# One w_mod tile kept on chip, and eleven row tiles of the up and gate gradients in other places: an adaLN decoder block, forward and backward

## The chip, the core and the metric

The kernel runs on one core of a Trainium2 chip. Its engines are PE (TensorE: matmuls and transposes), DVE (VectorE), ACT (ScalarE), POOL (GpSimd) and SP (SyncE). In this kernel POOL computes next to nothing: it issues most of the transfers between DRAM and SBUF, in program order, and SP issues the rest. The time is that of one execution on the device in microseconds; three executions are given, and their median is the figure.

## The reference, cut to what matters

One token (batch 1, sequence 1, D = 1024) goes through a block whose norms are modulated by a condition vector c, and all gradients are returned beside the output.

```python
mod = (silu(c) @ w_mod).reshape(1, 6, 1, -1)          # w_mod: 1024 x 6144
sa, ca, ga, sb, cb, gb = (mod[:, i] for i in range(6))
h = layernorm(x) * (1 + ca) + sa
x = x + ga * attention(h, k_cache, v_cache, wq, wo)    # 32 heads on 4 kv heads, last 4096 of 65536 positions
h = layernorm(x) * (1 + cb) + sb
x = x + gb * ((sigmoid(h @ w_gate) * (h @ w_up)) @ w_down)   # F = 3584
out, vjp = jax.vjp(f, A_x, k_cache, v_cache, wq, wo, w_gate, w_up, w_down, c, w_mod)
return (out, *vjp(grad_out))
```

The results are the output, a row for x and for c, and full gradients of k_cache, v_cache (1 x 4 x 65536 x 128 each, zero but for the last 4096 positions), wq (1024 x 4096), wo (4096 x 1024), w_up and w_gate (1024 x 3584 each), w_down (3584 x 1024) and w_mod (1024 x 6144), all in bf16. Most of these are outer products of two vectors, made on chip and written out.

## The kernel before, in words

**Storage.** One tile, `arena` (192 KiB of each of the 128 partitions), holds everything large. `ar(off, size)` is a piece of it by KiB; such an offset is called a place here. Every place is used several times in the course of the kernel, and an instruction that writes to a place waits until the earlier readers of those bytes, a store to DRAM among them, are done. Small vectors are tiles of their own, from `vt` (L107). `zeros` (L114) is a 2 KiB tile that feeds the first fills with zeros, `junk`, `scr` and `b1k` are 2 KiB tiles of scratch. `ones_f` (L126) is a 128 x 128 matrix of ones, the stationary operand of the sums over partitions in `total_bcast` (L289) and `layernorm_bwd_col` (L318); c_ps (L1382) reads one column of it.

**Order.** The schedule is written by hand (`manual_schedule`): each engine runs its instructions in program order. Transfers issued by POOL run in one queue, those by SP in another; both share the 16 transfer engines. The zero regions of the k_cache and v_cache gradients, most of the volume written, are cut into pieces of about 1 MB, and `zero(n, after)` puts n of them into POOL's queue, in the N loop and the B chunks each tied to a recent matmul, so that they go out at the matmuls' pace. The tables `Z_...` at the top say how many stand where. None is left after L1328.

**Stages.** w_mod's first two sections, k, wq and v are loaded; scores, softmax and the attention follow. The N loop (L720) runs 128 steps s, four groups of 32: every second step DVE scales two blocks of v, PE multiplies with k. The B chunks (`bch`) multiply with wo, which stays on chip as `wo_t` (places 160, 168, 176, 184, 64, 72, 80, 88). Then the modulations ga, cb, sb and gb are made from sections of w_mod, the FFN runs over seven blocks of F, forward and backward (`turn`, L1143), and the tail makes and stores the gradients.

**gb and its tiles.** Section 5 of w_mod (gb) is used twice: for gb itself, gb = silu(c) @ section 5, and at the end for the gradient of c, in `sec` (L1252). Its eight tiles `g_t[j]` (128 x 1024 bf16, 0.25 MiB each) are at places 48 to 58 for j = 0 to 5; j = 6 goes into the tile `zeros` at step s = 40, once the fills read their zeros from DRAM. For j = 7 there was no place that stays free: it is loaded to place 160 before the N loop (L561), its share of gb is summed at s = 24 and s = 26 (`mod_gb((7,))`, L744, and `gb_cols`, L747), and then wo_t[0] is loaded over it. The shares of the other seven follow at L1028 and are added. In the tail `sec_load(7)` (L1400) loads the tile a second time, into the last quarter of `sec_t[7]`, between sec(3) and sec(4).

**Row tiles.** `dw_rows(k, j, off, outer)` (L1123) makes one row tile of the gradient of w_up (k = 0) or w_gate (k = 1): DVE multiplies dug_row[k] by the column h2[:, j] into 7 KiB at place off, and POOL stores the 896 KiB. There are sixteen, from L1206 to L1397. Between them stand `dwo(u)` (L1258), which writes the gradient of wo over wo_t[u], and `sec(j)`, which makes 8 KiB of w_mod's gradient at the place of `sec_t[j]` (0, 8, 152, 16, 32, 40, 48, 56). Behind them `grad_kv` makes the gradients of v at places 64 to 95 and of k at 96 to 127, `dwq_tile` those of wq at places 184, 0, 8, 152, 32, 40, 16, 48, and `s2` those of w_mod's first two sections at 164, 24, 28, 56, 60, 168, 172, 128.

Of the kernel before, what the change touches and what calls it, by code (L numbers as in the profile page):

```python
# [10 lines left out]
P = 128  # L11
# [8 lines left out]
D = 1024  # L20
# [41 lines left out]
def kernel(  # L62
# [40 lines left out]
    def ar(off, size):  # L103
        return arena[:, int(off * KIB):int((off + size) * KIB)]


    def vt(shape, name, dt=FP32):  # L107
        return pool.tile(shape, dt, name=name)

    ctx.enter_context(tc.manual_schedule())  # L110

# [11 lines left out]
    ident_f = vt([P, P], "ident_f")  # L123
    make_identity(nc, ident_bf)
    make_identity(nc, ident_f)
    ones_f = vt([P, P], "ones_f")  # L126
    nc.vector.memset(ones_f, 1.0)

    def fill_rows(og, g):
# [158 lines left out]

    def total_bcast(part, ncol, name, scale):  # L289
        ps = new_acc("tot_" + name)  # L290
        nc.tensor.matmul(ps[:, 0:ncol], lhsT=ones_f[:, :], rhs=part[:, 0:ncol], start=True, stop=True)
        tot = vt([P, ncol], name)
        ts(tot, ps[:, 0:ncol], float(scale), ALU.mult)
        return tot
# [23 lines left out]
    def layernorm_bwd_col(dln, ln, rstd, name, gap=lambda: None):  # L318
        part = vt([P, 2], name + "_parts")
        nc.vector.reduce_sum(out=part[:, 0:1], in_=dln, axis=AX.X)  # L320
        tmp = vt([P, KD], name + "_tmp")
        ttr(tmp, dln, ln, part[:, 1:2])
        ps = new_acc("tot_" + name)
        nc.tensor.matmul(ps[:, 0:2], lhsT=ones_f[:, :], rhs=part[:, 0:2], start=True, stop=True)
# [52 lines left out]
    def wm_sec(sct, j, n, off, eng=nc.gpsimd):  # L377
        eng.dma_start(out=ar(off, 2 * n).rearrange("p (j x) -> p j x", j=n),
                            in_=wm_view[:, j:j + n, sct * D:(sct + 1) * D])
# [64 lines left out]
    def heads(w):  # L444
        return w.rearrange("p (n d) -> p n d", d=P)
# [105 lines left out]
    for ch in range(8):  # L551
# [5 lines left out]
        nc.scalar.copy(out=P_bf[:, ch * 512:(ch + 1) * 512], in_=ps[:, :])  # L557
        nc.vector.reduce_max(out=mx8[:, ch:ch + 1], in_=ps[:, :], axis=AX.X)
        zero(Z_KC[ch], mm)
    g_t = [ar(o, 2) for o in (48, 50, 52, 54, 56, 58)] + [zeros.bitcast(BF16), ar(160, 2)]  # L560
    wm_sec(5, 7, 1, 160)  # L561
    load_wo(2)
    load_wo(1)
    mx = vt([P, 1], "mx")
# [131 lines left out]
    jobs.clear()  # L696

    dffn_bf = vt([P, KD], "dffn_bf", BF16)
    gb_rest = vt([P, KD], "gb_rest")

    def mod_gb(ts_):
        ps = new_bank("g_ps")
        for t in ts_:
            rows_mm(ps, cs_bf[:, t:t + 1], heads(g_t[t]), t == ts_[0], t == ts_[-1])

        def cols():
            rows_to_cols(gb if ts_[0] == 7 else gb_rest, ps, KD, b1k)
            if ts_[0] != 7:
                addv(gb, gb, gb_rest)
        return cols  # L710

    ok4 = ok_sums()

# [6 lines left out]
    for g in range(G):  # L720
        nbank = bank_pair("n_ps", g)
        for t_ in range(KT):
            s = g * KT + t_
            vp = vp_t[(s // 2) % 2]
            if t_ % 2 == 0:
                tt(vp.rearrange("p t h d -> p (t h d)"),
                   v_nat[:, g, t_ * DH:(t_ + 2) * DH].rearrange("p (t o d) -> p t o d", t=2, o=1).broadcast_to([P, 2, HG, DH]),
                   pT2[:, g, HG * t_:HG * t_ + 2 * HG, :].rearrange("p n (o k) -> p n o k", o=1).broadcast_to([P, 2 * HG, 64, 2]),
                   ALU.mult)
            for k in range(2):  # L730
                mm = nc.tensor.matmul(nbank[k][:, :], lhsT=k_nat[:, g, t_ * DH:(t_ + 1) * DH],  # L731
                                      rhs=vp[:, t_ % 2, 4 * k:4 * k + 4, :].rearrange("p h d -> p (h d)"),
                                      start=(t_ == 0), stop=False)
            zero(Z_N[s], recent(mm, 6), True)
            if t_ == 20:
                build_bd(g)
            if s == 2:
                ok_cols(ok4)
            elif s == 4:
                ok_rows()  # L740
            elif s == 6:
                shuffle_o()
            elif s == 24:
                gb_cols = mod_gb((7,))  # L744
                load_wo(0)
            elif s == 26:
                gb_cols()  # L747
            elif s == 40:
                nc.gpsimd.dma_start(out=g_t[6], in_=wm_view[:, 6, 5 * D:6 * D])
# [275 lines left out]
    assert not bq  # L1025
    park(4, ppq, "pq")
    zero(Z_FOLD[1])
    mod_gb((0, 1, 2, 3, 4, 5, 6))()  # L1028
    mulv(dffn_bf, go_col, gb)
    bcast(dffn_bf, KD, b1k, "AV")  # L1030
    vT_unit = [tr_unit(v_nat[:, i // 4, (i % 4) * 1024:(i % 4 + 1) * 1024]) for i in range(16)]
# [10 lines left out]
    nc.vector.memset(fg, 0.0)  # L1042
    gu_ps, ffn_ps, dh2_ps = fg[:, 0:256], fg[:, 256:256 + KD], fg[:, 272:272 + JT]
    ffn = vt([P, KD], "ffn")
    gu_t = gb_rest

    def ffn_rows(out, col, w, stop):
        for a in range(4):
# [197 lines left out]
    dcs = vt([P, KD], "dcs")  # L1246
    late = [junk[:, i * P:(i + 1) * P] for i in range(8)]

    def sec_load(j):
        nc.gpsimd.dma_start(out=sec_t[j][:, 3 * D:4 * D], in_=wm_view[:, j, 5 * D:6 * D])  # L1250

    def sec(j):  # L1252
        w5 = g_t[j] if j < 7 else sec_t[j][:, 3 * D:4 * D]
        ttr(w5, w5, dmod_b4[:, 3 * D:4 * D], dcs[:, j:j + 1])
        outer_dve(sec_t[j], cs_col[:, j:j + 1], dmod_b4)
        nc.gpsimd.dma_start(out=dwm_view[:, j, 2 * D:6 * D], in_=sec_t[j])
# [78 lines left out]
    for h in range(HQ):  # L1335
        nc.tensor.matmul(dq_ps[:, h:h + 1], lhsT=N_sb[:, h * P:(h + 1) * P], rhs=do_bf[:, h:h + 1], start=True, stop=True)
    dwo(5)
    dq_bf = vt([P, HQ], "dq_bf", BF16)
    cp(dq_bf, dq_ps[:, 0:HQ])
    dug_rows(1)  # L1340
# [3 lines left out]
    dw_rows(0, 4, 32, outer_dve)  # L1344
    zero(Z_ROWS[2])
    dwo(3)
    dw_rows(0, 5, 64, outer_dve)
    dw_rows(0, 6, 72, outer_dve)
    zero(Z_ROWS[3])
    dw_rows(0, 7, 80, outer_dve)  # L1350
    for p in range(5):
        nc.scalar.copy(out=B_t[p], in_=BT_ps[p][:, :])
    dh1_ps = new_acc("dh1_ps")
# [4 lines left out]
    rot[:] = [(psum, "mm"), (pna, "na"), (pgu, "gu"), (ppq, "pq"), (px, "x"), (pna, "na"), (prq, "rq")]  # L1358
    nrot[0] = len(rot) - 1
    bcast(dmod_bf[:, 16:48], 32, dmod_b4, "A")  # L1360
    dw_rows(1, 0, 88, outer_dve)
    zero(Z_ROWS[4])
    dw_rows(1, 1, 40, outer_dve)
    dwo(1)
    dh1 = vt([P, KD], "dh1")
    cp(dh1[:, 0:NBP], dh1_ps[:, 0:NBP])
# [6 lines left out]
    dw_rows(1, 2, 16, outer_dve)  # L1373
    zero(Z_ROWS[5])
    dw_rows(1, 3, 32, outer_dve)
# [8 lines left out]
    crow = vt([P, 1], "crow")  # L1384
    cp(crow, c_ps[:, 0:1])
    sec(0)
    dw_rows(1, 4, 40, outer_dve)
    zero(Z_ROWS[6])
    sec(1)
    dw_rows(1, 5, 16, outer_dve)  # L1390
    for run in vT_unit[12:]:
        run()
    rebuild_P()
    bcast(dq_bf, HQ, dq_b, "A")
    dw_rows(1, 6, 32, outer_dve)
# [115 lines left out]
```

## Time and profile before

| | us |
|---|---|
| three executions | 593.43, 594.07, 594.16 |
| median | 594.07 |
| the profiled execution | 593.93 |
| its span, first to last instruction | 592.1 |

| engine | busy us | share of the span | instructions |
|---|---|---|---|
| PE, matmuls | 421.1 | 71% | 4167 |
| PE, weight loads | 243.2 | 41% | 4196 |
| DVE | 354.7 | 60% | 647 |
| ACT | 248.0 | 42% | 398 |
| POOL | 151.4 | 26% | 251 |

All times in the views are microseconds from the start of the span. The DMA share is the mean busy share of the 16 transfer engines; packets of two queues overlap in the records, so that it can be over 1. "A <- B" behind an instruction means that it stood idle until B was done. The time to landing of a transfer runs from its issue to its last completion, the time in the queue with it. Matmul ends are modelled, and a few per cent of the matmul records can be missing.

### The profile page before, as it was taken

Reading aid. Unit: us, or ns where it says so; the run is one execution under the profiler, and the core shown is the slowest. Engines: PE = TensorE matmul, PEld = TensorE weight load, DVE = VectorE, ACT = ScalarE, POOL = GpSimd, SP = SyncE. Lnnn points to the kernel's source line nnn. Section 1 sums busy time; section 2 is a strip of 40 time slices with the busy share of each in tenths; the row PEclk is TensorE's granted clock in tenths of the full one; section 3 lists DMA queues with packets and bytes.
Section 4 is the critical chain, followed back from the end, with each engine's and each line's share of the span. In section 5 each row is a group of like instructions: output and inputs, shape, how many; then the busy total and the mean of one; then the engine's idle time right before and its main releaser. Section 6 shows DMA issues by size and latency. Waiting matters only on the chain.

```text
span 592.1 us, 10185 instructions
## 1 busy us (share of the span) xinstructions
PE 421.1 (71%) x4167; PEld 243.2 (41%) x4196; DVE 354.7 (60%) x647; ACT 248.0 (42%) x398; POOL 151.4 (26%) x251
## 2 busy tenths in 40 slices
PE   3997679999999999997976756776665408275410
PEld 2784433322334545543444545555452307113100
DVE  3665679988830102039372876887986826696750
ACT  2579511554540103411123655666671426464310
POOL 3113213122122212122232321334222813133100
PEclk9998889999999999999997767778777657755555
DMA  8999999999999999999999999999999999999997
GB/s 347 423 418 422 424 462 427 425 431 425 426 401 452 419 445 426 408 419 438 427 390 407 418 411 408 399 410 402 422 420 427 424 427 421 424 404 413 412 415 321
DMA packets 31983, 246.32 MB, mean 416 GB/s; under 512 B 4781, under 2 KB 4781, under 8 KB 16624
## 3 DMA queue, kind: packets, MB, share of 16 engines
q0 software_dynamic: 26944, 226.25, 94.9%
q1 hardware_dynamic: 4944, 19.41, 9.4%
q8 instruction: 33, 0.54, 0.4%
q14 instruction: 14, 0.11, 0.1%
q10 hardware_dynamic: 48, 0.01, 0.0%
HBM read 88.78 MB, written 185.60 MB: 463 GB/s over the span
## 4 chain that ended last, share of the span: by engine, by line
DMA 34%; PE 26%; DVE 17%; issue 9%; ACT 8%; POOL 2%; ACTq 0%; POOLq 0%; DVEq 0%
DMA out_dram<-out_dram 13%; DMA out_dram<-arena 9%; PE n_ps L731 9%; DMA arena<-in_w_mod_dram 6%; DMA arena<-in_B_w_gate_dram 5%; DVE arena L246 4%; PE b_ps L792 4%; PE t_ps L679 4%; DVE scr L246 3%; DVE arena L242 3%; ACT arena L1295 2%; ACT arena L517 2%; DVE arena L229 2%; ACT arena L687 1%; PE tp_k L496 1%
## 5 line engine op out<-in xcount | busy, mean ns | idle before, releaser
L792 PE MATMUL b_ps<-arena 128*128 128x512 bf16 x493 | 114.3, 379 | 2.4 <-ACT arena L936 1.1
L229 DVE TENSOR_TENSOR arena<-arena 128x2048 bf16<-128x2048 bf16 x64 | 77.7, 1224 | 9.0 <-PE n_ps L731 5.3
L936 ACT COPY arena<-tp_side 128x1024 bf16<-128x1024 bf16 x62 | 60.9, 1017 | 49.7 <-PE tp_side L935 49.0
L792 PEld LDWEIGHTS <-arena 128*128 128x128 bf16 x512 | 48.3, 98 | 56.6 <-issue 2.9
L731 PE MATMUL n_ps<-arena 128*128 128x512 bf16 x246 | 66.2, 388 | 4.1 <-DVE arena L229 3.4
L193 POOL DMA_DIRECT2D out_dram<-out_dram x72 | 35.7, 496 | 127.2 <-PE n_ps L731 50.8
L935 PE MATMUL tp_side<-ident_bf,arena 128*128 128x128 bf16 x496 | 50.5, 268 | 10.2 <-DVE arena L229 5.8
L935 PEld LDWEIGHTS <-arena 128*128 128x128 bf16 x496 | 41.8, 123 | 19.1 <-issue 9.0
L687 ACT CAST arena<-t_ps 128x512 bf16<-128x512 f32 x56 | 28.9, 598 | 39.9 <-PE t_ps L679 39.9
L242 DVE TENSOR_SCALAR arena<-arena,h 128x3584 bf16<-128x3584 bf16 (+1 forms) x24 | 28.5, 1193 | 25.0 <-DMA out_dram<-arena 25.0
L1291 PE MATMUL ps_kv<-arena 32*128 32x512 bf16 x64 | 24.4, 588 | 24.9 <-DVE arena L250 14.4
L246 DVE CUSTOM_DVE_ANT_0 arena<-arena,scr 128x1024 bf16<-128x1024 bf16 x35 | 40.8, 1219 | 0.2
L1295 ACT ACTIVATE arena<-ps_kv 128x512 bf16<-128x512 f32 x48 | 25.4, 697 | 33.2 <-PE ps_kv L1291 33.0
L246 DVE CUSTOM_DVE_ANT_0 scr<-arena,b1k 128x1024 bf16<-128x1024 bf16 x28 | 34.2, 1222 | 3.4 <-DMA arena<-in_B_w_down_dram 3.0
L731 PEld LDWEIGHTS <-arena 128*128 128x128 bf16 x256 | 21.4, 99 | 35.8 <-issue 19.4
L238 DVE CAST arena<-b_ps 128x512 bf16<-128x512 f32 x6 | 4.1, 691 | 48.8 <-PE b_ps L792 48.8
L200 POOL DMA_DIRECT2D out_dram<-out_dram x32 | 19.5, 610 | 32.6 <-DVE rows_all L229 24.4
L679 PE MATMUL t_ps<-arena 128*32 128x512 bf16 x256 | 24.1, 399 | 3.4 <-ACT arena L756 2.8
L517 ACT COPY arena<-tp_wq 128x1024 bf16<-128x1024 bf16 x23 | 21.4, 1070 | 7.3 <-PE tp_wq L515 7.3
L1291 PEld LDWEIGHTS <-arena 32*128 32x128 bf16 x64 | 6.9, 116 | 41.1 <-issue 40.4
L1073 ACT COPY arena<-tp_ug 128x1024 bf16<-128x1024 bf16 x21 | 20.5, 1007 | 7.0 <-PE tp_ug L1072 7.0
L961 POOL DMA_DIRECT2D arena<-in_B_w_up_dram x14 | 10.8, 771 | 39.6 <-DVE dh2acc L246 21.1
(330 smaller groups left out, 671.8 us busy)
## 6 DMA issues: line engine op xcount, KB each, us to landing
out_dram<-arena POOLq DMA_DIRECT2D x35, 1024.0 KB, 12.2
out_dram<-out_dram POOLq DMA_DIRECT2D x32, 1024.0 KB, 12.8
out_dram<-arena POOLq DMA_DIRECT2D x16, 896.0 KB, 12.7
out_dram<-zeros POOLq DMA_DIRECT2D x10, 1024.0 KB, 10.7
arena<-in_A_wq_dram POOLq DMA_DIRECT2D x8, 1024.0 KB, 21.1
arena<-in_A_wo_dram POOLq DMA_DIRECT2D x8, 1024.0 KB, 13.5
arena<-in_w_mod_dram POOLq DMA_DIRECT2D x7, 1024.0 KB, 18.9
arena<-in_B_w_up_dram POOLq DMA_DIRECT2D x14, 512.0 KB, 9.8
```

Of the source, the lines that this page charges most:

```text
L193: ins = nc.gpsimd.dma_start(out=as_rows(region, BIGP).bitcast(FP32), in_=zero_src[:, 0:P * ZW // 4].rearrange("i (p x) -> (i p) x", p=BIGP ...
L229: return nc.vector.tensor_tensor(out=out, in0=a, in1=b, op=op)
L242: return nc.vector.tensor_scalar(out=out, in0=a, scalar1=s1, scalar2=None, op0=op0)
L246: return nc.vector.tensor_tensor_reduce(out=out, in0=w, in1=b, scale=1.0, scalar=0.0, op0=ALU.mult, op1=ALU.add, accum_out=acc)
L517: nc.scalar.copy(out=blk, in_=tp[:, :])
L679: nc.tensor.matmul(ps[32 * hh:32 * hh + 32, :].rearrange("p (j m) -> p j m", j=4), lhsT=N_sb[:, h * P + a:(h + 1) * P - 3 + a:4], rhs=a4[: ...
L687: nc.scalar.copy(out=o, in_=v)
L731: mm = nc.tensor.matmul(nbank[k][:, :], lhsT=k_nat[:, g, t_ * DH:(t_ + 1) * DH], rhs=vp[:, t_ % 2, 4 * k:4 * k + 4, :].rearrange("p h d -> ...
L792: mm = nc.tensor.matmul(bbank[p][k][:, :], lhsT=a4[:, p, h, :], rhs=wo_t[u][:, a, k * 512:(k + 1) * 512], start=(i == 0 and a == 0), stop= ...
L935: nc.tensor.transpose(tp[:, i * P:(i + 1) * P], blk[:, i * P:(i + 1) * P], ident_bf[:, :])
L936: nc.scalar.copy(out=blk if dst is None else dst, in_=tp[:, :])
L1295: nc.scalar.activation(out=o, in_=v, func=ACT.Copy, scale=float(scale))
```

## The change

- `vt` gives vectors of at most 48 words out of one tile, `slab` (728 fp32 words), one behind the other; larger ones stay tiles of their own. Before the last vectors of the tail the slab is set anew to 1.75 KiB at place 146.25.
- `ones_f` is one column, read as a 128 x 128 matrix by a repeated column.
- `g_t[7]` is a tile of its own, `g_last`. Its load before the N loop and `sec_load(7)` go, and it is loaded in the N loop at s = 44.
- `mod_gb` sums all eight tiles at once, where it summed seven; the part at s = 24 and 26 goes. `gu_t`, which shared a tile with the partial sum, has one of its own.
- Eleven of the sixteen row tiles are made in other places. The order of the instructions stays.

| row tile | 0,5 | 0,6 | 0,7 | 1,0 | 1,1 | 1,2 | 1,3 | 1,4 | 1,5 | 1,6 | 1,7 |
|---|---|---|---|---|---|---|---|---|---|---|---|
| place before | 64 | 72 | 80 | 88 | 40 | 16 | 32 | 40 | 16 | 32 | 40 |
| place after | 176 | 160 | 40 | 64 | 72 | 80 | 16 | 32 | 88 | 160 | 40 |

```diff
+    slab = [pool.tile([P, 728], FP32, name="slab"), 0]
     def vt(shape, name, dt=FP32):
-        return pool.tile(shape, dt, name=name)
+        n = shape[1] if dt == FP32 else (shape[1] + 1) // 2
+        if dt not in (FP32, BF16) or n > 48:
+            return pool.tile(shape, dt, name=name)
+        a = slab[1]
+        slab[1] += n
+        v = slab[0][:, a:a + n]
+        return v if dt == FP32 else v.bitcast(BF16)[:, 0:shape[1]]
...
-    ones_f = vt([P, P], "ones_f")
+    ones_f = vt([P, 1], "ones_f")
...
-        nc.tensor.matmul(ps[:, 0:ncol], lhsT=ones_f[:, :], rhs=part[:, 0:ncol], start=True, stop=True)
+        nc.tensor.matmul(ps[:, 0:ncol], lhsT=ones_f[:, 0:1].broadcast_to([P, P]), rhs=part[:, 0:ncol], start=True, stop=True)
...
-    g_t = [ar(o, 2) for o in (48, 50, 52, 54, 56, 58)] + [zeros.bitcast(BF16), ar(160, 2)]
-    wm_sec(5, 7, 1, 160)
+    g_t = [ar(o, 2) for o in (48, 50, 52, 54, 56, 58)] + [zeros.bitcast(BF16), vt([P, D], "g_last", BF16)]
...
-    def mod_gb(ts_):
+    def mod_gb():
         ps = new_bank("g_ps")
-        for t in ts_:
-            rows_mm(ps, cs_bf[:, t:t + 1], heads(g_t[t]), t == ts_[0], t == ts_[-1])
-
-        def cols():
-            rows_to_cols(gb if ts_[0] == 7 else gb_rest, ps, KD, b1k)
-            if ts_[0] != 7:
-                addv(gb, gb, gb_rest)
-        return cols
+        for t in range(KD):
+            rows_mm(ps, cs_bf[:, t:t + 1], heads(g_t[t]), t == 0, t == KD - 1)
+        rows_to_cols(gb, ps, KD, b1k)
...
             elif s == 24:
-                gb_cols = mod_gb((7,))
                 load_wo(0)
-            elif s == 26:
-                gb_cols()
-            elif s == 40:
-                nc.gpsimd.dma_start(out=g_t[6], in_=wm_view[:, 6, 5 * D:6 * D])
+            elif s in (40, 44):
+                j = 6 + (s - 40) // 4
+                nc.gpsimd.dma_start(out=g_t[j], in_=wm_view[:, j, 5 * D:6 * D])
...
-    mod_gb((0, 1, 2, 3, 4, 5, 6))()
+    mod_gb()
...
-    gu_t = gb_rest
+    gu_t = vt([P, KD], "gu_t")
...
-    def sec_load(j):
-        nc.gpsimd.dma_start(out=sec_t[j][:, 3 * D:4 * D], in_=wm_view[:, j, 5 * D:6 * D])
-
     def sec(j):
-        w5 = g_t[j] if j < 7 else sec_t[j][:, 3 * D:4 * D]
+        w5 = g_t[j]
...
     dwo(5)
+    slab[:] = [ar(146.25, 1.75).bitcast(FP32), 0]
...
-    dw_rows(0, 5, 64, outer_dve)
-    dw_rows(0, 6, 72, outer_dve)
+    dw_rows(0, 5, 176, outer_dve)
+    dw_rows(0, 6, 160, outer_dve)
     zero(Z_ROWS[3])
-    dw_rows(0, 7, 80, outer_dve)
+    dw_rows(0, 7, 40, outer_dve)
...
-    dw_rows(1, 0, 88, outer_dve)
+    dw_rows(1, 0, 64, outer_dve)
     zero(Z_ROWS[4])
-    dw_rows(1, 1, 40, outer_dve)
+    dw_rows(1, 1, 72, outer_dve)
...
     sec(3)
-    sec_load(7)
```

More of the change, by code (lines that the diff above doesn't have):

```diff
@@ L104, in ar @@
         return arena[:, int(off * KIB):int((off + size) * KIB)]
+    slab = [pool.tile([P, 728], FP32, name="slab"), 0]
     def vt(shape, name, dt=FP32):
-        return pool.tile(shape, dt, name=name)
+        n = shape[1] if dt == FP32 else (shape[1] + 1) // 2
[3 more added lines that the diff above has]
+        slab[1] += n
+        assert slab[1] <= slab[0].shape[1], slab
+        v = slab[0][:, a:a + n]
+        return v if dt == FP32 else v.bitcast(BF16)[:, 0:shape[1]]
     ctx.enter_context(tc.manual_schedule())
@@ L323, in layernorm_bwd_col @@
         ps = new_acc("tot_" + name)
-        nc.tensor.matmul(ps[:, 0:2], lhsT=ones_f[:, :], rhs=part[:, 0:2], start=True, stop=True)
+        nc.tensor.matmul(ps[:, 0:2], lhsT=ones_f[:, 0:1].broadcast_to([P, P]), rhs=part[:, 0:2], start=True, stop=True)
         gap()
@@ L698 @@
     dffn_bf = vt([P, KD], "dffn_bf", BF16)
-    gb_rest = vt([P, KD], "gb_rest")
-    def mod_gb(ts_):
+    def mod_gb():
         ps = new_bank("g_ps")
-        for t in ts_:
-            rows_mm(ps, cs_bf[:, t:t + 1], heads(g_t[t]), t == ts_[0], t == ts_[-1])
-        def cols():
-            rows_to_cols(gb if ts_[0] == 7 else gb_rest, ps, KD, b1k)
-            if ts_[0] != 7:
-                addv(gb, gb, gb_rest)
-        return cols
+        for t in range(KD):
+            rows_mm(ps, cs_bf[:, t:t + 1], heads(g_t[t]), t == 0, t == KD - 1)
+        rows_to_cols(gb, ps, KD, b1k)
     ok4 = ok_sums()
@@ L1372 @@
     pd = b1k.bitcast(FP32)[:, 0:HQ]
-    dw_rows(1, 2, 16, outer_dve)
+    dw_rows(1, 2, 80, outer_dve)
     zero(Z_ROWS[5])
-    dw_rows(1, 3, 32, outer_dve)
+    dw_rows(1, 3, 16, outer_dve)
     dcs234 = matvec_T(lambda jb, nb: w2_t[jb][:, nb * P:(nb + 1) * P], dh2_hl, "dcs234")
@@ L1386 @@
     sec(0)
-    dw_rows(1, 4, 40, outer_dve)
+    dw_rows(1, 4, 32, outer_dve)
     zero(Z_ROWS[6])
     sec(1)
-    dw_rows(1, 5, 16, outer_dve)
+    dw_rows(1, 5, 88, outer_dve)
     for run in vT_unit[12:]:
@@ L1394 @@
     bcast(dq_bf, HQ, dq_b, "A")
-    dw_rows(1, 6, 32, outer_dve)
+    dw_rows(1, 6, 160, outer_dve)
     zero(Z_ROWS[7])
```

## The prediction

> **What bounds the kernel now.** I read the page first: the span, and the volume that the DMA engines moved. Then a table of stretches, for the busy time of each engine, the DMA share and the rate.
>
> ```profile
> span 592.1 us, 10185 instructions
> ...
> DMA packets 31983, 246.32 MB, mean 416 GB/s; under 512 B 4781, under 2 KB 4781, under 8 KB 16624
> ```
> ```profile
> core 0: us, PE busy (x) PEld busy (x) DVE busy (x) ACT busy (x) POOL busy (x), PEclk, DMA share, GB/s
> 60.00:200.00 140.00, 126.91 (x838) 49.96 (x856) 92.16 (x106) 51.90 (x124) 32.36 (x62) 0.97 1.05 428
> 200.00:330.00 130.00, 111.92 (x933) 61.52 (x936) 48.86 (x105) 33.55 (x43) 32.12 (x55) 0.97 1.04 422
> 330.00:440.00 110.00, 75.46 (x1108) 61.16 (x1109) 88.22 (x184) 66.95 (x88) 32.41 (x49) 0.72 1.14 410
> 440.00:496.00 56.00, 23.35 (x358) 18.04 (x357) 37.09 (x92) 21.46 (x27) 23.70 (x26) 0.66 1.05 425
> 496.00:516.00 20.00, 9.64 (x141) 7.20 (x142) 10.60 (x15) 11.06 (x18) 2.66 (x5) 0.79 1.02 424
> 516.00:536.00 20.00, 13.53 (x50) 4.94 (x50) 18.40 (x34) 13.23 (x28) 6.80 (x10) 0.50 1.00 408
> 536.00:588.00 52.00, 14.31 (x100) 5.59 (x96) 26.42 (x49) 11.37 (x21) 6.84 (x12) 0.50 1.01 413
> 588.00:592.10 4.10, 0.00 (x0) 0.00 (x0) 0.00 (x0) 0.00 (x0) 0.00 (x0) 0.50 0.19 80
> ```
>
> The last three columns are the granted TensorE clock, the DMA share and GB/s. The share is 1.00 or more in every stretch up to 588 us, whatever the compute engines do: PE is busy 127 of 140 us in one stretch and 14 of 52 in another, and the rate stays between 408 and 428 GB/s. So the transfers never run out, and the end is the sum of the bytes over the rate, plus a start and a last landing. An engine that waits costs nothing as long as the transfers in the queue outlast its wait. Whether they do in the tail, where the row tiles are moved, is told by the waits of DVE (us in total, times, longest) and by the time from issue to landing of the stores there: those issued from 462 to 515 us first, then those from 515 to 535.
>
> ```profile
> DVE arena L242 <- DMA out_dram<-arena: 30.7, 12, 7.0
> ```
> ```profile
> out_dram<-arena POOLq DMA_DIRECT2D x12, 896.0 KB, 13.7
> out_dram<-arena POOLq DMA_DIRECT2D x9, 1024.0 KB, 14.4
> ```
> ```profile
> out_dram<-arena POOLq DMA_DIRECT2D x8, 1024.0 KB, 8.4
> out_dram<-arena POOLq DMA_DIRECT2D x1, 896.0 KB, 7.3
> arena<-in_w_mod_dram POOLq DMA_DIRECT2D x1, 256.0 KB, 8.4
> ```
>
> DVE stands 30.7 us in the tail, twelve times, because the place it wants to write is still being stored. But a store lands 7.3 to 14.4 us after its issue, so between three and six stores stand in the queue (1 MB at 424 GB/s takes 1.049/0.424 = 2.47 us). The longest wait, 7.0 us, did not empty it.
>
> **The change part by part.** *One load less.* The tile j = 7 of the gb section of w_mod (128 x 1024 bf16, 0.262 MB) was loaded at about 54 us and again at about 522 us; now it is loaded once, at step s = 44 of the N loop, where tile 6 is loaded at s = 40. The early load and the new one first, by the issues on POOL around them (start, duration, line, what it waited for):
>
> ```profile
> 54.09 0.56 POOL L378 DMA_DIRECT2D arena<-in_w_mod_dram  x1 [1.06 <-PE sc_ps L554]
> 58.30 1.06 POOL L375 DMA_DIRECT2D arena<-in_A_wo_dram  x2 [3.65 <-PE sc_ps L554]
> 66.81 0.54 POOL L202 DMA_DIRECT2D out_dram<-zeros  x1 [7.45 <-DVE rsum L587]
> ```
> ```profile
> 98.90 0.57 POOL L749 DMA_DIRECT2D zeros<-in_w_mod_dram  x1
> 101.04 0.50 POOL L193 DMA_DIRECT2D out_dram<-out_dram  x1 [1.57 <-PE n_ps L731]
> ```
>
> Both stand in the stretch of 428 GB/s, so each takes 0.262/0.428 = 0.6 us of the transfers. The early one leaves, -0.6 us; the new one enters a little after 101 us, +0.6 us; the two cancel if the queue holds transfers all the way between. The risk is at 58 to 67 us, where POOL waits 3.65 and 7.45 us for PE and DVE: if the queue ran dry there the early gain would be worth nothing. The share of 1.05 says no, so I take 0, with +0.6 us as the far end.
>
> The late load is dearer than its bytes. This is its issue, and the stretch in 4 us slices:
>
> ```profile
> 521.57 0.55 POOL L1250 DMA_DIRECT2D arena<-in_w_mod_dram  x1
> ```
> ```profile
> 512.00:516.00 4.00, 0.00 (x0) 0.00 (x0) 1.10 (x2) 0.00 (x0) 0.20 (x1) 0.50 1.02 426
> 516.00:520.00 4.00, 0.00 (x0) 0.00 (x0) 4.00 (x7) 0.00 (x0) 1.06 (x2) 0.50 1.00 415
> 520.00:524.00 4.00, 1.83 (x6) 0.51 (x6) 3.93 (x11) 1.23 (x3) 1.08 (x2) 0.50 1.00 409
> 524.00:528.00 4.00, 4.00 (x12) 1.21 (x11) 4.00 (x5) 4.00 (x9) 1.55 (x2) 0.50 0.97 373
> 528.00:532.00 4.00, 4.00 (x10) 0.82 (x9) 4.00 (x5) 4.00 (x10) 1.55 (x2) 0.50 1.01 420
> 532.00:536.00 4.00, 3.70 (x26) 2.39 (x25) 2.47 (x10) 4.00 (x10) 1.55 (x2) 0.50 1.02 422
> ```
>
> It lands 8.4 us after its issue, at 521.57 + 8.4 = 530.0 us, so its reads run in the slices from 520 to 530. There the rate falls to 409 and 373 GB/s against about 420 around it: (5 + 11 + 47) GB/s x 4 us = 0.25 MB not moved from 516 to 528, or 0.60 us at 420. With its own bytes, 0.262/0.42 = 0.62 us, the load costs 1.2 us. The lower bound is the bytes alone, 0.6. The upper bound puts all that the transfers lose after 516 us on it: 20 x (424 - 408)/424 = 0.75 us, 52 x (424 - 413)/424 = 1.35 us, and 0.62, together 2.7 us. I take 1.2, since the dip stands where the load stands, and the slices right behind it are back at 420.
>
> The Trainium skill, "DMA: Bandwidth & Descriptors", section "Anatomy of one DMA — SWDGE (gpsimd) path", fits one transfer as about 2.0 us fixed plus its bytes at 436 GB/s; an estimate by it is 2.6 us for this load, and the sum by it would be near 591.5. In this trace only 1.2 us can be seen at the load itself, as if most of a fixed part lay under the neighbours.
>
> *The rows of gb are summed in one go.* At s = 24 and 26 four matmuls and two DVE instructions go; four matmuls join the 28 at 315 us, and an add goes.
>
> ```profile
> 92.61 0.42 DVE L229 TENSOR_TENSOR b1k<-g_ps,rows_all 128x256 f32<-128x256 f32 x1
> 93.06 0.42 DVE L442 TENSOR_REDUCE mod_col<-b1k 128x8 f32<-128x256 f32 x1
> ```
> ```profile
> 296.78 18.79 DMA arena<-in_w_mod_dram
> ...
> 315.62 1.07 PE g_ps L433 x28
> ...
> 317.63 0.18 DVE mod_col L229
> ```
>
> DVE is spared 0.84 us near 93 us. At 315 us the chain gets 4 x 1.07/28 = 0.15 us longer and 0.18 us shorter. Both lie under transfers (shares 1.05 and 1.04): 0, and 0.2 us either way without that cover.
>
> *Eleven row tiles move.* No instruction is added; only the place written, and with it the store that must have landed, changes. Counting transfers on POOL's queue between that store and the new tile: up dw_rows 5, 6 and 7 go from 6, 6, 6 to 8, 8, 12; gate 0 to 7 from 5, 14, 9, 8, 4, 4, 4, 3 to 9, 9, 10, 10, 10, 13, 10, 10; sec(3) and sec(4) behind them from 3 and 3 to 7 and 6. So almost every tile finds its place free by the time POOL can take its store, and most of the 30.7 us leaves the stretch from 470 to 520. What is late next is tile s2(3) at place 56, which waits for the store of sec(7) and does not move in the queue:
>
> ```profile
> 558.31 0.75 DVE L242 TENSOR_SCALAR arena<-arena,cs_col 128x2048 bf16<-128x2048 bf16 x1 [4.21 <-DMA out_dram<-arena]
> ```
>
> DVE arrives there sooner and waits longer than 4.2 us. With the share at 1.00 all of this is worth 0 in time; if a fuller queue raised the 408 GB/s of 516 to 536 us, that is inside the 2.7 us above.
>
> *Small vectors in one slab, ones_f as one column.* Two instructions at the start get smaller; those that read the vectors keep shape and order, and waits stay by ranges as in the arena. Each stands under transfers: 0.
>
> The sum: -0.6 + 0.6 - 1.2 = -1.2 us. The profiled execution took 593.93 us (span 592.1 and 1.8 around it), so it would take 592.7. The median shown, 594.07, is 0.14 above that execution: 592.8.
>
> **The rivals.** *(A) Only the bytes count:* the dip from 516 to 528 has another cause (it begins at 516, before the load is issued), or the early gain is lost at 58 to 67 us. Then -0.6 us: 593.4. For it speaks 415 GB/s in a slice that ends before 521.57; against it that the deepest slice, 373, is the one before the landing.
>
> *(B) The late load upsets, or the thin queue slows, the whole rest:* all of the loss after 516 us goes with the load and the fuller queue, -2.7 us: 591.4. For it: 413 GB/s holds to 588. Against it: a load of 0.6 us of bytes would have to be felt for 52 us. The skill's fixed 2.0 us would come out about here.
>
> *(C) Slower: POOL becomes the bound of the tail.* With DVE no longer standing still from 470 to 520 us, its writes fall together with POOL's issues, and each issue gets longer. The row of POOL's sec stores (min, median, max ns) shows what an issue can take:
>
> ```profile
> L1256 POOL DMA_DIRECT2D out_dram<-arena x8: 532/776/1019, 500.5 to 540.9; - x8
> ```
>
> If some 24 issues took 1019 instead of 532 ns, POOL would lose 24 x 0.49 = 11.7 us. It decides from the point where that exceeds the 8.4 us that the queue holds: 3.3 us dry, less 1.2: 596.2. Against it: POOL is busy 6.80 of 20 us there. The Trainium skill, "SBUF — State Buffer", section "SBUF: two separate sides", says that a DVE instruction in a two-port mode locks GpSimd out, which then cannot write descriptors while the transfer engines idle; that speaks against filling DVE's pauses, and the trace shows 0.5 us of it at most, with no idle transfers.
>
> **How the numbers follow.** Forecast (-0.8 to -2.0) 0.47, A 0.23, B 0.20, C 0.10. A difference of 0.2%, 1.2 us, is about what a measurement of this kernel can tell from no change, so faster means under 592.9 and slower over 595.3. B is faster; the forecast straddles the border, somewhat more than half of it below; A is the same; C is slower: faster 0.50, same 0.40, slower 0.10. The range runs from B's 591.4 to just past the time of before, 594.4, which leaves out C and what exceeds B.
>
> **What would show it.** The page's volume falls from 246.32 to 246.06 MB. The 4 us slices near 524 us keep 410 or more. DVE's wait for stores at L242 falls well below 30.7 us, and the one before s2(3) grows. Stores issued between 462 and 535 us land later after their issue than 14 and 8 us, since the queue is fuller. The share stays at 1.00 to the end; a slice of the tail below 0.95 would prove me wrong, as would an end that moves while rate and bytes do not explain it.

## The result and the profile after

| | before | after |
|---|---|---|
| median, us (22 runs each) | 593.73 | 592.92 |
| lowest to highest | 593.11 to 594.16 | 592.20 to 594.03 |
| ratio, 95% interval | | 0.9986, 0.9980 to 0.9992 |
| the profiled execution | 593.93 | 593.15 |

The changed kernel is 0.8 us faster, with 0.5 to 1.2 us inside the interval. The forecast was 1.2 us and 592.8. The page of after first, for span and volume:

```profile
span 591.4 us, 10184 instructions
...
DMA packets 31903, 246.05 MB, mean 416 GB/s; under 512 B 4765, under 2 KB 4765, under 8 KB 16544
```

The volume fell by one tile, 246.32 to 246.05 MB, and the mean rate is the same 416 GB/s. Before and after name the two kernels from here on. The table of stretches of after, with the columns of the prediction (the last two are DMA share and GB/s), for the tail:

```profile
440.00:496.00 56.00, 28.59 (x448) 22.78 (x446) 43.23 (x100) 25.47 (x31) 19.07 (x27) 0.63 1.05 425
496.00:516.00 20.00, 6.13 (x65) 2.91 (x62) 13.26 (x22) 5.14 (x10) 5.25 (x8) 0.72 1.01 424
516.00:536.00 20.00, 15.28 (x76) 5.38 (x75) 10.04 (x18) 15.92 (x34) 4.66 (x6) 0.50 1.02 421
536.00:588.00 52.00, 13.59 (x73) 4.88 (x69) 26.36 (x49) 11.03 (x20) 6.84 (x12) 0.50 1.00 409
...
520.00:524.00 4.00, 3.27 (x7) 0.69 (x7) 0.00 (x0) 3.92 (x9) 0.00 (x0) 0.50 1.01 418
524.00:528.00 4.00, 4.00 (x9) 0.79 (x8) 3.90 (x5) 4.00 (x10) 1.55 (x2) 0.50 1.01 424
528.00:532.00 4.00, 4.00 (x10) 0.80 (x9) 2.44 (x6) 4.00 (x10) 1.55 (x2) 0.50 1.01 418
...
568.00:580.00 12.00, 0.00 (x0) 0.00 (x0) 2.00 (x4) 0.00 (x0) 1.05 (x2) 0.50 1.02 416
584.00:588.00 4.00, 0.00 (x0) 0.00 (x0) 0.00 (x0) 0.00 (x0) 0.00 (x0) 0.50 0.83 345
```

Up to 516 us the rates are those of before (425 and 424 GB/s). From 516 to 536 the rate is 421 where it was 408: 20 x 13/421 = 0.62 us gained, and the slice from 524 to 528 us moves 424 GB/s where it moved 373. The 409 of the last long stretch (413 before) is no slower transfer: it holds the end of the stream, which comes earlier, so that 584 to 588 is only partly filled (345). Where both kernels still have work, from 568 to 580 us, it is 416 here and was 410.

The waits, where the forecast expected DVE's to shrink. DVE's wait for stores in the tail of after, in all (us, times, longest), and the instructions with the long ones:

```profile
DVE arena L251 <- DMA out_dram<-arena: 25.4, 10, 6.5
```
```profile
510.66 1.29 DVE L251 TENSOR_SCALAR arena<-arena,slab 128x4096 bf16<-128x4096 bf16 x1 [6.48 <-DMA out_dram<-arena]
...
524.10 2.48 DVE L251 TENSOR_SCALAR arena<-arena,slab 128x4096 bf16<-128x4096 bf16 x2 [5.25 <-DMA out_dram<-arena]
...
557.63 0.75 DVE L251 TENSOR_SCALAR arena<-arena,slab 128x2048 bf16<-128x2048 bf16 x1 [4.35 <-DMA out_dram<-arena]
```

30.7 us became 25.4. Before row tiles DVE waits 7.8 us in all where it waited 25.0; new are 11.9 us before 8 KiB tiles of sec, and the wait before s2(3) is still there. POOL's waits between 468 and 516 us, of before and then of after:

```profile
POOL out_dram L1126 <- DVE arena L242: 20.5, 7, 5.4
POOL out_dram L1256 <- DVE arena L242: 6.9, 2, 5.1
```
```profile
POOL out_dram L1126 <- DMA out_dram<-arena: 9.0, 5, 2.2
POOL out_dram L1126 <- DVE arena L251: 6.4, 4, 1.6
POOL out_dram L1258 <- DMA out_dram<-arena: 3.5, 2, 1.9
POOL out_dram L1253 <- DMA out_dram<-arena: 1.6, 1, 1.6
```

POOL waited 27.4 us in these two rows for tiles that DVE had not made. Now it waits 14.1 us until an earlier transfer has landed, and still 16.3 us for DVE (6.4 in the row shown, the rest in smaller ones). Counted from issues and landings, seven or eight of POOL's transfers, 6.6 to 8.3 MB, stand between issue and landing all the time from 468 to 513 us; in before it was four to eight. That it is never more than eight is the program's doing: in the traces of before and after POOL's transfers report their landing on eight semaphores in turn (numbers 110 to 117), and from 469 to 512 us every issue of after waits for the semaphore of the transfer eight before it. How much the queue itself could hold isn't shown. The stores take longer to land accordingly; those issued from 462 to 515 us of after, then those from 515 to 535:

```profile
out_dram<-arena POOLq DMA_DIRECT2D x13, 896.0 KB, 17.6
out_dram<-arena POOLq DMA_DIRECT2D x11, 1024.0 KB, 17.4
```
```profile
out_dram<-arena POOLq DMA_DIRECT2D x6, 1024.0 KB, 13.5
```

They were 13.7 and 14.4, and 8.4.

### The profile page after: what moved, and what is told of

It is laid out like the page before. It is cut to its first block, busy times and chain, and to the rows that moved or that the text cites. A ratio compares the mean times of both kernels' runs of the same rounds, so it can differ in the third digit from the quotient of the medians.

```text
span 591.4 us, 10184 instructions
## 1 busy us (share of the span) xinstructions
PE 426.5 (72%) x4167; PEld 245.7 (42%) x4196; DVE 353.6 (60%) x644; ACT 247.9 (42%) x398; POOL 147.3 (25%) x250
## 2 busy tenths in 40 slices
DMA packets 31903, 246.05 MB, mean 416 GB/s; under 512 B 4765, under 2 KB 4765, under 8 KB 16544
## 4 chain that ended last, share of the span: by engine, by line
DMA 36%; PE 27%; DVE 18%; ACT 9%; issue 5%; POOL 1%; ACTq 0%; POOLq 0%; DVEq 0%
DMA out_dram<-out_dram 13%; DMA out_dram<-arena 10%; PE n_ps L733 9%; DMA arena<-in_w_mod_dram 6%; DMA arena<-in_B_w_gate_dram 6%; DVE arena L255 5%; PE b_ps L792 4%; DVE arena L251 4%; PE t_ps L687 4%; DVE scr L255 3%; ACT arena L1292 3%; ACT arena L526 2%; DVE arena L238 2%; ACT arena L695 1%; PE tp_k L505 1%
## 5 line engine op out<-in xcount | busy, mean ns | idle before, releaser
L238 DVE TENSOR_TENSOR arena<-arena 128x2048 bf16<-128x2048 bf16 (+1 forms) x67 | 78.2, 1177 | 9.0 <-PE n_ps L733 5.2
L251 DVE TENSOR_SCALAR arena<-arena,slab 128x3584 bf16<-128x3584 bf16 (+2 forms) x40 | 43.4, 1120 | 24.1 <-DMA out_dram<-arena 24.1
L1288 PE MATMUL ps_kv<-arena 32*128 32x512 bf16 x64 | 26.6, 581 | 28.5 <-DVE arena L259 11.7
L1049 PE MATMUL fg<-arena,slab 128*32 128x256 bf16 x224 | 15.1, 404 | 8.2 <-DMA arena<-in_B_w_gate_dram 8.2
## 6 DMA issues: line engine op xcount, KB each, us to landing
arena<-in_A_wo_dram POOLq DMA_DIRECT2D x8, 1024.0 KB, 13.7
```

What stands on the lines that cost most here:

```text
L238: return nc.vector.tensor_tensor(out=out, in0=a, in1=b, op=op)
L251: return nc.vector.tensor_scalar(out=out, in0=a, scalar1=s1, scalar2=None, op0=op0)
L1288: nc.tensor.matmul(ps[:, :], lhsT=rows[r, t8 * P:(t8 + 1) * P], rhs=bd[r, :], start=True, stop=True, tile_position=(32 * tc_, 0))
```

## The experiments

Two theories were compared. *The load:* the late load of tile 7 costs its bytes (0.62 us) and the dip from 516 to 528 us (0.60 us), as forecast, and the places are worth nothing. *The thin queue:* the dip comes from stores that are issued late, because the tiles wait for their places, so that too little is left in the queue; then the places are worth the dip, and the load only its bytes.

All ratios below are against the kernel before, run on the same chip; 0.0001 is 0.06 us. Intervals of 95% are some 0.001 either way, 0.6 us, so a single ratio doesn't part the theories: the rows do, and the repetition.

### Undoing one half

**Old places.** The changed kernel, with the eleven row tiles in their places of before, once and a second time beside the others.

```diff
-    dw_rows(0, 5, 176, outer_dve)
-    dw_rows(0, 6, 160, outer_dve)
+    dw_rows(0, 5, 64, outer_dve)
+    dw_rows(0, 6, 72, outer_dve)
...
-    dw_rows(1, 5, 88, outer_dve)
+    dw_rows(1, 5, 16, outer_dve)
...
-    dw_rows(1, 6, 160, outer_dve)
+    dw_rows(1, 6, 32, outer_dve)
```

> The changed kernel with the eleven row tiles back in their old places; everything else as changed. If only the transfers count (theory Q), the places are worth nothing: the time is that of the changed kernel, 0.8 us under the kernel before (ratio about 0.9986), while DVE's waits for stores return to about 30 us. If the fuller queue of the new places made the gain (theory M), the time goes back to the kernel before (ratio 1.000).

> The late load is gone, the eleven tiles are in their old places. Thin queue: the slice from 524 to 528 us stays under 380 GB/s with a share under 0.95, and the time is 593.3 to 593.6, 0.4 to 0.6 us over the changed kernel. Load: 592.8 to 593.0, as the changed kernel, with no such slice.

Measured: 593.5 us, 0.9993 (0.9984 to 1.0002), and again 593.25 us, 0.9995 (0.9986 to 1.0004). The slices of the first of the two:

```profile
520.00:524.00 4.00, 1.62 (x6) 0.52 (x6) 3.93 (x11) 1.02 (x2) 0.53 (x1) 0.50 1.00 414
524.00:528.00 4.00, 4.00 (x11) 1.16 (x10) 4.00 (x7) 4.00 (x10) 1.55 (x2) 0.50 0.87 360
528.00:532.00 4.00, 4.00 (x9) 0.80 (x8) 4.00 (x5) 4.00 (x10) 1.55 (x2) 0.50 1.02 420
```

There is no late load in this kernel, and the dip is deeper than in the kernel before: 360 GB/s at a share of 0.87 (373 at 0.97 before). The second execution has the same two numbers. A share a little over 1 is a full one: POOL's queue alone reaches 101.6% in the view of before from 462 to 515 us. So 0.87 beside 1.01 is (1.01 - 0.87) x 4 = 0.56 us in which the transfer engines stood idle, an estimate; taken in half microseconds the share is 0.67, 0.62 and 0.74 from 525.5 to 527.0 us. As a cause of the dip the load falls here. The packets of before say the same: the load's 64 packets of 4 KB run from 526.1 to 529.5 us, half of them in the slice of 373 GB/s, half in the next one at 420, and none in the slices of 415 and 409.

What the queue held can be counted: the volume moved after a time, less what is issued after it, was waiting at that time. This is the view of transfers from 526 us to the end, of before (bytes moved; then stores issued or being issued, KB each):

```profile
DMA packets 4239, 25.96 MB, mean 393 GB/s; under 512 B 528, under 2 KB 528, under 8 KB 1616
...
out_dram<-arena POOLq DMA_DIRECT2D x16, 1024.0 KB, 12.6
out_dram<-arena SPq DMA_DIRECT2D x4, 1024.0 KB, 18.9
out_dram<-arena SPq DMA_DIRECT2D x6, 512.0 KB, 9.0
out_dram<-arena POOLq DMA_DIRECT2D x2, 512.0 KB, 18.7
```

Twenty stores of 1.049 MB and eight of 0.524 are 25.17 MB, so 0.79 MB was left, 1.9 us at 420 GB/s, beside the store of sec(4), whose issue was running. The same view of the kernel with the old places, and of after:

```profile
DMA packets 4158, 25.73 MB, mean 390 GB/s; under 512 B 507, under 2 KB 507, under 8 KB 1531
...
out_dram<-arena POOLq DMA_DIRECT2D x16, 1024.0 KB, 10.8
```
```profile
DMA packets 4144, 25.62 MB, mean 388 GB/s; under 512 B 507, under 2 KB 507, under 8 KB 1531
...
out_dram<-arena POOLq DMA_DIRECT2D x14, 1024.0 KB, 14.3
```

With the old places and no late load 25.73 - 25.17 = 0.56 MB was left; in after, with two stores fewer still to issue, 25.62 - 23.07 = 2.55 MB. So the late load of before, with its 0.26 MB, stood in the thin place and filled part of it. POOL's issues there show why it is thin, in the kernel with the old places (start, duration, what POOL waited for):

```profile
516.56 0.53 POOL L1126 DMA_DIRECT2D out_dram<-arena  x1 [4.14 <-DVE arena L251]
519.15 0.53 POOL L1253 DMA_DIRECT2D out_dram<-arena  x1 [2.06 <-issue]
521.24 0.53 POOL L1253 DMA_DIRECT2D out_dram<-arena  x1 [1.55 <-DVE arena L247]
525.54 1.02 POOL L1253 DMA_DIRECT2D out_dram<-arena  x1 [3.77 <-DVE arena L251]
```

Between sec(3) at 521.24 and sec(4) at 525.54 nothing is issued for 4.3 us. Such a gap makes no dip by itself. In after nothing is issued from 518.00 us to the store of sec(5), 7.7 us later, and the rate holds, since the queue is deep enough:

```profile
525.68 1.02 POOL L1253 DMA_DIRECT2D out_dram<-arena  x1 [7.14 <-DVE arena L251]
```

**Places only.** The kernel before, with only the eleven places changed, so that both loads of tile 7 stay; twice as well.

```diff
-    dw_rows(0, 5, 64, outer_dve)
-    dw_rows(0, 6, 72, outer_dve)
+    dw_rows(0, 5, 176, outer_dve)
+    dw_rows(0, 6, 160, outer_dve)
...
```

> The kernel before with the eleven row tiles in the new places and nothing else changed. Theory Q: no difference (ratio 1.000 within 0.0005), DVE's waits fall to about 25 us and the stores of the tail stand 17 us in the queue. If the late load cost more than its bytes only because the queue was thin (8.4 us), the dip near 525 us shrinks and about 0.5 us is gained (ratio 0.9990). Theory M: all of the gain, ratio 0.9986.

> The kernel before with the eleven tiles in their new places, and with both loads of tile 7. Thin queue: 593.1 to 593.4, 0.4 to 0.6 us under the kernel before. Load: 593.7, as the kernel before.

Measured: 592.95 us, 0.9990 (0.9981 to 0.9999), and 593.58 us, 0.9996 (0.9987 to 1.0006). The first has a gain that can be told from none, the second has not: it lies outside the 593.1 to 593.4 of the thin queue, nearer to the 593.7 of the load. The slices of the first:

```profile
516.00:520.00 4.00, 0.00 (x0) 0.00 (x0) 2.26 (x3) 0.44 (x1) 1.55 (x2) 0.50 1.00 411
520.00:524.00 4.00, 3.79 (x8) 0.80 (x8) 0.37 (x1) 4.00 (x10) 0.00 (x0) 0.50 1.02 421
524.00:528.00 4.00, 4.00 (x9) 0.79 (x8) 4.00 (x5) 4.00 (x10) 1.55 (x2) 0.50 1.00 399
528.00:532.00 4.00, 4.00 (x10) 0.79 (x8) 1.97 (x6) 4.00 (x10) 1.55 (x2) 0.50 1.02 426
```

With the load kept and the queue full, 373 becomes 399, at a share of 1.00: no idle engines, but 25 GB/s under after. The second has 398 at 1.01. So the load does seem to have a dip of its own, 4 x (424 - 399) = 0.10 MB or 0.24 us, less than half of what the forecast gave it; this is an upper figure, for half of its packets run in the next slice, at 426 GB/s.

**The changed kernel again,** as the mark for the second runs.

> The changed kernel once more, beside the next three. Both theories take it as the mark: about 592.9 us, 0.8 us under the kernel before, and no 4 us slice between 516 and 536 us under 410 GB/s. The theory of the thin queue says that of the 0.8 us the places bring some 0.4 to 0.6 and the load that goes 0.6, less what is lost on the way; the theory of the load says that the load brings nearly all of it.

Measured: 592.73 us, 0.9987 (0.9978 to 0.9995), with 422 GB/s from 524 to 528 us. Four differences give each half: the places are worth 0.0010 and 0.0004 (before to places only) and 0.0007 and 0.0008 (old places to after), on average 0.0007 or 0.4 us; the load 0.0007 and 0.0005, 0.0004 and 0.0009, on average 0.0006 or 0.4 us. All eight have the same sign, though they share kernels and only the first is clear of noise by itself. What is called the load here is all of the change but the places, the slab and gb in one go with it. A least-squares fit to the 165 single times of the four kernels gives 0.40 us for the places and 0.35 for the rest, about 0.2 us either way at 95% if the executions are independent. Both halves are there; in size they can't be told apart. The profiled executions show the part of the places in the rate from 516 to 536 us:

| GB/s from 516 to 536 us | first | again |
|---|---|---|
| before | 408 | |
| old places, no late load | 407 | 404 |
| new places, late load kept | 417 | 417 |
| after | 421 | 422 |

With the load kept the places raise it by 9 GB/s, 20 x 9/420 = 0.43 us. The load alone, taken away at the old places, raises nothing.

**Two places only.** The changed kernel with old places for nine tiles, and new ones for the two that stood at 16 and 32, the places of sec(3) and sec(4). The edit is shown against the kernel with all the old places.

```diff
-    dw_rows(1, 5, 16, outer_dve)
+    dw_rows(1, 5, 88, outer_dve)
...
-    dw_rows(1, 6, 32, outer_dve)
+    dw_rows(1, 6, 160, outer_dve)
```

> The changed kernel with only two of the eleven tiles in new places, gate tile 5 at 88 and gate tile 6 at 160, so that sec(3) and sec(4) find places 16 and 32 free; the other nine are in their old ones. Thin queue at sec(3) and sec(4): DVE's waits in front of sec(3) and sec(4) go, sec(4)'s store is issued 3 us or more earlier than with the old places (525.3 us), the slice from 524 to 528 us is 400 GB/s or more, and the time is that of the changed kernel, 592.9. If the places matter only as a whole, or not at all: 593.4, as with the old places, and the slice stays under 380.

Measured: 593.22 us, 0.9992 (0.9984 to 1.0001), and this slice:

```profile
524.00:528.00 4.00, 4.00 (x12) 1.24 (x11) 4.00 (x5) 4.00 (x9) 1.55 (x2) 0.50 0.89 369
```

The expectation missed. DVE did not wait in front of sec(3) and sec(4) in the first place: in before it works without a pause from 514.90 us until sec(4) is made. The two tiles in new places no longer wait, but the wait moved to the next one, gate tile 7 at place 40, on DVE and so on POOL:

```profile
514.88 1.15 DVE L251 TENSOR_SCALAR arena<-arena,slab 128x3584 bf16<-128x3584 bf16 x1 [5.80 <-DMA out_dram<-arena]
```
```profile
509.37 0.53 POOL L1126 DMA_DIRECT2D out_dram<-arena  x1 [0.17 <-issue]
516.33 0.53 POOL L1126 DMA_DIRECT2D out_dram<-arena  x1 [6.43 <-DVE arena L251]
...
525.32 1.02 POOL L1253 DMA_DIRECT2D out_dram<-arena  x1 [3.77 <-DVE arena L251]
```

sec(4)'s store is issued at 525.32 as before (525.33), and the dip stays. DVE's wait in the tail is 29.6 us in nine pieces where it was 29.8 in twelve with all the old places. The premise, that places 16 and 32 set when sec(4) is issued, was wrong: gate tile 7, which waits for place 40, and DVE's work behind it set it. That the dip goes with the late issue agrees with the thin queue, but this run was no test of it.

### The price of a load

**Early instead of at s = 44.** The changed kernel, with its one load of tile 7 put where the early load was.

```diff
+    nc.gpsimd.dma_start(out=g_t[7], in_=wm_view[:, 7, 5 * D:6 * D])
     load_wo(2)
...
-            elif s in (40, 44):
-                j = 6 + (s - 40) // 4
-                nc.gpsimd.dma_start(out=g_t[j], in_=wm_view[:, j, 5 * D:6 * D])
+            elif s == 40:
+                nc.gpsimd.dma_start(out=g_t[6], in_=wm_view[:, 6, 5 * D:6 * D])
```

> The changed kernel with the one load of tile 7 issued before the N loop, where the first load stood, and not at s = 44. Theory Q: a load costs its 0.6 us wherever it stands while the queue holds transfers, so the time is that of the changed kernel (ratio 0.9986 within 0.0005). If the queue runs dry at 58 to 67 us, the early load is free and 0.6 us more is gained (ratio 0.9976).

Measured: 592.88 us, 0.9984 (0.9975 to 0.9993), the time of after. Early or at s = 44 is the same, as the forecast's -0.6 + 0.6 has it. The interval just reaches the 0.9976 of a queue that runs dry, so the time alone doesn't exclude it; the trace of before does, with shares of 1.05 to 1.16 and 413 to 431 GB/s in the 4 us slices from 52 to 68 us.

**Four loads more.** Four unread tiles of 0.262 MB, put behind sec(3) in the changed kernel and in the kernel before, and before the N loop in the changed one; and one unread load of the same 1.05 MB in all behind sec(3), in rows of 8 KB instead of 2 KB.

```diff
     sec(3)
+    for i in range(4):
+        nc.gpsimd.dma_start(out=ar(168 + 2 * i, 2), in_=wm_view[:, i, 5 * D:6 * D])
```

> The changed kernel with four more loads of 0.262 MB each, read by nobody, right behind sec(3), where the late load stood; there the queue now holds 16 us. If a late load costs its bytes alone, +4 x 0.62 = +2.5 us against the changed kernel (595.4). If it costs the 1.2 us that I read from the dip, whatever the queue holds, +4.8 us (597.7). If the extra came from the thin queue only, +2.5 us here and more in the next.

> The kernel before with the same four extra loads right behind the late load; there the queue holds 8 us. Bytes alone: +2.5 us against the kernel before (596.2). 1.2 us each: +4.8 us (598.5). Extra from the thin queue: clearly more than in the run with the full queue.

> The changed kernel with four more loads of 0.262 MB each ahead of the N loop, where the first load stood. If the queue never runs dry from there on, +4 x 0.6 = +2.4 us against the changed kernel (595.3). If there is slack at 58 to 67 us or in the N loop, less, down to 0 (592.9).

> The changed kernel with one load of 1.05 MB (the bytes of the four, in rows of 8 KB) where the late load stood. Bytes alone: +2.5 us (595.4). If the extra is paid per transfer, +2.5 + 0.6 = +3.1 us (596.0), and less than with four loads; if it is paid per byte read among stores, as much as with the four: +4.8 us (597.7).

Measured, in four to seven executions each:

| | us | ratio | against its own base | each load |
|---|---|---|---|---|
| after, 4 late | 596.56 | 1.0042 (1.0027 to 1.0057) | 0.0056, 3.3 us | 0.8 us |
| before, 4 late | 596.89 | 1.0050 (1.0035 to 1.0065) | 0.0050, 3.0 us | 0.7 us |
| after, 4 early | 595.61 | 1.0029 (1.0017 to 1.0041) | 0.0043, 2.6 us | 0.6 us |
| after, one of 1.05 MB late | 595.90 | 1.0035 (1.0024 to 1.0047) | 0.0049, 2.9 us | |

The base of "after" is 0.9986. An early load costs its bytes (0.262/0.42 = 0.62 us). A late one costs 0.1 to 0.2 us more by these ratios (their intervals leave some 0.2 us for each load), and not the 1.2 us of the forecast; it costs no more at the thin queue of before than at the full one of after. With four of them the dip is there at a full queue; the slices of the changed kernel with four late loads:

```profile
524.00:528.00 4.00, 4.00 (x10) 0.84 (x9) 3.97 (x5) 4.00 (x9) 1.39 (x2) 0.50 0.99 352
528.00:532.00 4.00, 4.00 (x10) 0.85 (x9) 2.37 (x6) 4.00 (x10) 1.19 (x3) 0.50 0.98 337
```

The engines are busy (0.99 and 0.98) but move less. Against 424 and 418 of after that is 4 x (72 + 81) = 0.61 MB or 1.5 us for four, some 0.4 us for each, as an upper figure, since slices behind may give some back. So there are two kinds of dip, told apart by the share: in these runs reads in the tail lower the rate of busy engines, and a thin queue leaves them idle. The single load in larger rows dips as well, 377 and 360 GB/s in these slices, so that short rows alone aren't the cause; what it is, these runs don't tell.

### A version that might beat both

The fills of zeros that read them from DRAM, all as 16 rows of 64 KB, for the stretch from 330 to 440 us with its 410 GB/s at a share of 1.14.

```diff
-            elif big and region.shape[0] == 1:
+            elif (big or from_dram[0]) and region.shape[0] == 1:
```

> The changed kernel with all zero fills that read DRAM made as 16 pieces of 64 KB rows, also the 32 of 8 KB rows from 186 us on. Landings of the two kinds follow each other by 2.42 us (64 KB rows) and about 2.45 us (8 KB rows). Theory Q: the sum of the spacings counts, 32 x 0.03 = 1 us less than the changed kernel at most (ratio against the kernel before 0.997); if the long rows hold up the loads of the FFN stage, PE waits longer for weights and the time is the same or up to 1 us longer.

Measured: 592.94 us, 0.9988 (0.9979 to 0.9997): no gain over after. The stretch from 330 to 440 us has a share of 1.04 (1.14 in after) and moves 411 GB/s where it moved 410; the one from 440 to 496 us has 1.00 (1.05) and 418 (425). Larger rows lower the share here and bring no bytes. No kernel of the study beats the changed one by more than the intervals.

## Why the prediction was right, and where its steps failed

**The bound held.** Transfers set the end: after has 0.62 us less of bytes, the share is 1.00 or more in every stretch up to 580 us, and PE, DVE and ACT changed their busy times in the tail (DVE 18.40 to 10.04 of 20 us from 516 to 536); what of this reached the time came by the depth of the queue. "So the transfers never run out" went too far: the averages of stretches hid slices such as the one at 0.97. Each extra load in the experiments came out in the time with at least its bytes.

**The early load and the new one (0).** Right: one load put early or at s = 44 gives 0.9984 and 0.9986, and four loads put early cost their bytes.

**The late load (-1.2), the step that failed.** The forecast took 0.62 of bytes and 0.60 of a dip, "since the dip stands where the load stands", and let the load's reads run "in the slices from 520 to 530"; they run from 526.1 to 529.5 us. With the load gone and the old places kept the dip stayed and deepened (360 GB/s, share 0.87), which only rival A had allowed for, with its remark that the dip begins before the load is issued. Taken away at the old places, the load brings about 0.4 us: its 0.62 us of bytes go, and the engines stand idle 0.56 us where they stood idle (1.01 - 0.97) x 4 = 0.16 us before. That idle time explains some 17 of the 47 GB/s that the slice of 373 lacks, and the load's own dip at most 25; both are estimates. Four in a row cost 0.7 to 0.8 us each.

**The eleven row tiles (0), the other half of the same error.** "With the share at 1.00 all of this is worth 0 in time" was wrong: the places bring about 0.4 us, because they have stores in the queue at 524 us. The forecast read the depth of the queue off the time to landing: 7.3 to 14.4 us, "between three and six stores". The count of bytes says 0.79 MB at 526 us beside the store being issued, less than one store. The time to landing holds the transfer's own bytes, and more: the store issued at 525.33 us found about 0.79 MB + 0.67 us x 373 GB/s = 1.04 MB, and with its own 1.05 MB that is 5.0 us at 420 GB/s; it landed 7.0 us after its issue, so some 2 us, an estimate, are more than its bytes explain. By the packets, POOL's queue had moved as many bytes as were issued up to the end of this store 1.6 us before it landed; for the same store it is 1.6 us in after too, and 0.8 and 1.1 us in the two executions with the old places. The Trainium skill, "DMA: Bandwidth & Descriptors", section "Anatomy of one DMA — SWDGE (gpsimd) path", puts most of a fixed 2.0 us of a transfer into its completion, behind the last byte. Here such a part isn't fixed; how much of it lies behind the store's own last byte, and why it is shorter behind idle engines, stays open. The prediction cited the same fit as a price of a load. As a price it doesn't hold in a full queue (0.6 us for an early load, not 2.6); as a part of the time to landing it would have been a warning that 7.0 us aren't 7.0 us of bytes. The share of 0.97 in the slice of the dip, quoted in the prediction, was the sign of it.

**DVE's waits ("most of the 30.7 us leaves").** Off in size: 5.3 us left. Of the 25.0 us before row tiles 17.2 went, but with a fuller queue each place comes free later (17.6 us to landing for 13.7), so sec tiles and POOL's own issues wait instead. Here, and in the kernel with two new places, a wait that was taken away turned up at the next user of a place; what changed is the order of the waits, and with all eleven places the depth of the queue. That s2(3) would wait longer was right, 4.21 to 4.35 us, though by little.

**The sum (-1.2, measured -0.8).** That the forecast's total came out near is luck in part: it put the whole dip down to the load, and what does make the dip leaves with this change too, so that the wrong share doesn't show in the sum. In the tail of the profiled executions the 1.2 us are there: 0.62 us of bytes and 20 x 13/421 = 0.62 us of rate. Some of it may be given back earlier. The dwo store of 461.75 us, the same in both kernels, is issued 0.17 us later in after:

```profile
461.75 0.71 POOL L1261 DMA_DIRECT2D out_dram<-arena  x1 [0.97 <-DVE do_bf L238]
```
```profile
461.92 0.71 POOL L1258 DMA_DIRECT2D out_dram<-arena  x1 [0.97 <-DVE slab L247]
```

It was 0.32 us later in the second profile of after, and 0.09 us earlier in the kernel with the early load, whose time is yet the same. Single executions scatter by that much, so where the missing 0.4 us went stays open; the interval of the measured difference reaches to 1.2 us.

**The slab and ones_f, gb in one go (0).** Not tried by themselves. They are part of what is called the load's half above, 0.35 us with some 0.2 either way, so that the 0 given to them is neither shown nor refuted.

**The rivals.** *A (only bytes, -0.6)* was right on the dip's cause in part, and missed that another part of the change removes it. *B (-2.7)* needed a higher rate to the end; from 536 to 580 us the rate rose at most from 410 to 416 in a stretch, and 413 stayed 413 from 536 to 552. *C (POOL the bound)* did not come: POOL is busy 4.66 of 20 us from 516 to 536, less than the 6.80 before; between 468 and 516 us it waits for DVE or for the landing of the transfer eight before.

**What would show it.** Volume, slices near 524 us, longer landings and a share of 1.00 came as named, DVE's waits less so (above). One more is off: the slice from 584 to 588 us has 0.83, which is the end of the stream that comes earlier and not a gap in it.

## What to carry to other kernels

Read the depth of a transfer queue as bytes moved after a time less bytes issued after it, not from the time to landing, which holds the transfer's own bytes and a part in which nothing of it moves: here a store that took 7.0 us to land found about 1 MB ahead of it. Where transfers bound the kernel, a slice with a low rate at a share well under 1.00 wants earlier issues, and removing bytes from it lengthens the idle time (0.16 to 0.56 us here). A low rate at a share of 1.00 calls for other transfers, which no run here tried with success. Before an expected gain is put on one edit, look whether another edit of the same change touches the same slice.

## What the runs showed of the hardware

- At most eight of POOL's transfers, up to 8.3 MB, stood between issue and landing. The program's eight semaphores, used in turn, set that, and in after POOL waited 14.1 us for landings between 468 and 516 us.
- The store of sec(4) landed 0.8 to 1.6 us after POOL's queue had moved as many bytes as were issued up to its end: 1.6 in before and after, 0.8 and 1.1 with the old places, there right behind the idle engines.
- Four unread loads of 0.262 MB among stores lowered the rate to 352 and 337 GB/s in two slices at shares of 0.99 and 0.98, and one of 1.05 MB to 377 and 360; among the early traffic four cost no more than their bytes.
- Fills between DRAM and DRAM in rows of 64 KB took a lower share (1.04 for 1.14 from 330 to 440 us) and gave no more bytes in a us (411 and 410 GB/s).
